# Polysketch attention with hash routing on one core: 16-bit routing one-hots, tails in two products, the first batch in groups of four tiles, three buffers for q's features

## The chip, the cores and the metric

The kernel runs on one core of a Trainium2 chip. A core has five engines that run side by side[...]: TensorE (PE in the profile, with its weight loads as a row of their own, PEld), VectorE (DVE), ScalarE (ACT), GpSimd (POOL) and SyncE (SP). SP only issues DMAs here; POOL issues the indirect ones. The metric is the device time of one execution in microseconds (us). The kernel before took 212.41 us, the median of three runs (211.67 to 212.51). The profile is of one more execution, whose time was 205.21 us and whose instructions span 203.5 us. All starts and durations below are from that execution.

## What is computed

```python
# q, k, v: (4 batches, 4 heads, 1088 tokens, 32), S1, S2: (8, 32)
def phi(x):                         # 64 features of a token
    a = einsum('rd,bhsd->bhsr', S1, x)
    b = einsum('rd,bhsd->bhsr', S2, x)
    return einsum('bhsi,bhsj->bhsij', a, b).reshape(..., 64)
q_p, k_p = phi(q), phi(k)
kv  = einsum('bhsf,bhsd->bhfd', k_p, v)
z   = sum(k_p, axis=2)
num = einsum('bhsf,bhfd->bhsd', q_p, kv)
den = einsum('bhsf,bhf->bhs', q_p, z)[..., None] + 1e-6
x   = (num / den).transpose(0, 2, 1, 3).reshape(4352, 128)

expert = token_ids * 2654435761 % 8           # one expert of 8 for a token
for e in range(8):
    mask = expert == e
    out[mask] = relu(x[mask] @ w1[e]) @ w2[e] # (128 -> 1024 -> 128)
```

The multiplier is 1 modulo 8, so a token's expert is its id's last three bits.

## The kernel before, in words

**Names.** P is 128. A batch has T = 8 main tiles of 128 tokens and a tail of SP = 64 tokens. The tails of the four batches lie together in one tile, two to each half of the partitions. Q = 4 tiles form a group; GQ = 2 groups are a batch. FB = 2: the 64 features of a head are handled as two blocks of 32 (D) for q. DA = 33 is a head's 32 values and a one, which makes the denominator come out beside the numerator. ST = 36 lists of 128 tokens each hold the routed tokens (18, HT, from the early part of the tokens and 18 from all), and C = 34 is how many tokens a partition holds in the routing.

**Stage 1, attention, about 0 to 71 us.** For each batch b the engines do this, with the code's helpers named:

- SP loads k, q and v (`load_main`), two batches deep, and the tails (`load_tail`, four DMAs for each of k, v and q). The loads for all batches are issued from one list at the top, in the order k0, q0, v0, k1, the tails of k and v, q1, the tail of q, v1, and so on. SP takes them in order[...].
- PE turns k by transposing it against an identity (`transposed`, L353), ACT copies the result out of PSUM; PE multiplies with S (`k_products`, L362), ACT copies again (`copied`, L379). DVE forms k's features by a broadcast product (`k_features`, L385).
- DVE turns q in 32 by 32 blocks (`q_blocks`, L440), PE multiplies with S (`q_products`, L362), ACT copies, DVE forms q's features and turns them (`q_features` L385 and `q_turned` L460). Features of q live in tiles `fT`, two buffers.
- PE sums features times values over the eight tiles and the tail (`kv_products`, L413). ACT copies the diagonal blocks of the result in 16 pieces of 32 by 66 into the block matrices `m` (`kv_diagonal`, L434), which have zeros elsewhere. In the last batch, kv is first copied to SBUF (`kv_both`), and the 16 pieces are shared: 8 on ACT, 8 on DVE.
- PE multiplies q's features with `m` (`x_products`, L469), eight times for each group, and the tail of a batch by eight products that contract over only 32 rows each (`x_tail_products`, L480). fp32 products run as two passes on PE, so the profile counts two matmuls for each. ACT copies to `xe` (L472, L483). DVE takes reciprocals of the denominators (L493, L494), and POOL, for one batch in the middle and part of the last DVE, multiplies (`x_main`, L499; `x_tail`, L513) and SP writes the rows to a DRAM scratch, `x_rows`.

The routing is woven in on DVE: `route_scan` and `route_counts` in the first batch, `route_ranks` and `route_slots` in batch 0's loop, then `route_rows(b)` (L314), a one-hot of 128 columns for half of the 34 tokens of a partition, once in each of batches 0 and 1, and `route_tiles` (L318 to L321) after the loop: a one-hot of 36 columns, scaled by the partition number and by the column number. PE contracts row and tile one-hots into the list of tokens (`route_list`, L327). `route_end` makes the row numbers `get` and `put` of it.

**Stage 2, the handover, about 55 to 74 us.** The first six gathers of rows from `x_rows` (`fetch(0)`, `fetch(1)`, L586) are issued by POOL. They need `get` and the rows of the first two batches and of the first half of batch 2. `bring(k)` transposes three gathered tiles on PE (L627).

**Stage 3, the experts, 71.8 to 196 us.** 16 groups of 288 tokens: PE does `layer1` (L690) and `layer2` (L697) of neighbouring groups in turn, ACT and DVE evict, POOL gathers and scatters. `bring(1)` comes after the fourth of the eight products of the first group, `bring(2)` in the second group.

**What sets the order.** There is no planner: everything runs under a manual schedule, so each engine runs its instructions in the order in which the program lists them. A helper that is called earlier moves all that it issues forward on each of its engines, past what the others have queued there. Buffers turn in pools (`bufs=`): a tile that takes a used buffer waits for that buffer's readers. `keep_busy` (L178) issues idle matmuls at the start, WARM = 7 of them ahead of the first transposes.

Of the kernel before, what the change touches and what calls it, by code (L numbers as in the profile page):

```python
# [30 lines left out]
def kernel(  # L31
# [38 lines left out]
    WARM = 7  # L70
# [6 lines left out]
    hots = tc.alloc_tile_pool(name="hots", bufs=1)  # L77
    ps = ctx.enter_context(tc.tile_pool(name="ps", bufs=4, space=bass.MemoryType.PSUM))
# [18 lines left out]
    def load_tail(src, name, eng):  # L97
        t = const.tile([P, H, TT, D], F32, name=name)
        for b in range(B):
            u = b % 2  # L100
            eng.dma_start(t[u * SP:(u + 1) * SP, :, b // 2], src[b, :, SM:, :].rearrange("h p d -> p h d"))
        return t
# [16 lines left out]
    def load_batch(b):  # L119
        k_t.append(load_main(k, b, "k"))  # L120
        q_t.append(load_main(q, b, "q"))
        v_t.append(load_main(v, b, "v"))
# [17 lines left out]
    q_tail = load_tail(q, "q_tail", nc.sync)  # L140
# [6 lines left out]
    warm = const.tile([P, 512], BF16)  # L147
# [5 lines left out]
    for t in range(Q):  # L153
# [7 lines left out]
                            fill=0.0, base=0, channel_multiplier=-1)  # L161
    keep = const.tile([P, E, C], F32)
# [9 lines left out]
    def keep_busy(n):  # L172

        if n == 0:
            return
        p = ps_o.tile([P, 512], F32, tag="o", name="idle")
        for _ in range(n):
            nc.tensor.matmul(p[:], warm[:, 0:P], warm[:], start=True, stop=True)  # L178
# [6 lines left out]
    xes = [const.tile([P, GQ * H * Q + H, DA], F32, name=f"xe{i}") for i in range(2)]  # L185
    for m in ms[0] + ms[1]:
        nc.vector.memset(m[:], 0.0)
# [62 lines left out]
    st = const.tile([P, 2, C], F32)  # L250
# [35 lines left out]
    def route_slots():  # L286
# [22 lines left out]
        nc.vector.tensor_copy(st[:], st_i[:])  # L309


    def route_rows(part):
        c = slice(part * C // 2, (part + 1) * C // 2)
        nc.vector.tensor_tensor(row1[:, c], iota[:].unsqueeze(1).to_broadcast([P, C // 2, P]),  # L314
                                st[:, 1, c].unsqueeze(2).to_broadcast([P, C // 2, P]), op=OP.is_equal)

    def route_tiles():
        nc.vector.tensor_tensor(in_tile[:], iota[:, 0:ST].unsqueeze(1).to_broadcast([P, C, ST]),  # L318
                                st[:, 0].unsqueeze(2).to_broadcast([P, C, ST]), op=OP.is_equal)
        nc.vector.tensor_scalar(tiles[:, :, 0], in_tile[:], p1[:], None, op0=OP.mult)  # L320
        nc.vector.tensor_tensor(tiles[:, :, 1], in_tile[:], iota[:, 0:C].unsqueeze(2).to_broadcast([P, C, ST]),  # L321
                                op=OP.mult)
# [51 lines left out]
    def copied(ab_ps, rows=P, n=T):  # L374

        ab = work.tile([P, T, H, 2, R], F32, tag="ab", name="ab", bufs=3)
        for g in range(0, n, Q):
            w = min(Q, n - g)
            nc.scalar.copy(ab[:rows, g:g + w].rearrange("p t h x r -> p t h (x r)"),  # L379
                           ab_ps[:rows, g // Q, :, 0:w].rearrange("p h t y -> p t h y"))  # L380
        return ab
# [6 lines left out]
    def k_features(ab, n, pool, tag):  # L388

        kp = pool.tile([P, n, H, R, R], F32, tag="kp" + tag, name="kp" + tag, bufs=1)  # L390
        for g in range(0, n, Q):
            features(kp[:, g:min(n, g + Q)].rearrange("p t h i j -> p (t h) i j"),
                     ab[:, g:min(n, g + Q)].rearrange("p t h x r -> p (t h) x r"))
        return kp

    def values(vsrc, n, pool, tag, copy=nc.gpsimd.tensor_copy):
# [3 lines left out]
        copy(va[:, :, :, 0:D], vsrc[:].rearrange("p h t d -> p t h d"))  # L400
        return va

    def kv_products(b, main, tail, midway=None):
        kv = ps_o.tile([P, H // 2, HA + 2 * DA], F32, tag="o", name="kv")
        u = b % 2
        steps = [(main, t, slice(0, P)) for t in range(T)] + [(tail, b // 2, slice(u * SP, (u + 1) * SP))]
        for n, ((kp, va), t, rows) in enumerate(steps):
            if midway and n == T // 2:
                midway()
# [8 lines left out]
        return kv  # L418

    def kv_diagonal(b, kv):  # L420

        m = ms[b % 2]
        kv = kv[:, :, 0:2 * DA]
        if b > EB:
# [3 lines left out]
            kv = both  # L428
        for f in range(FB):
            copy = nc.vector.tensor_copy if b > EB and f else nc.scalar.copy  # L430
            for h in range(2):
                src = kv[h * R * R + f * D:h * R * R + (f + 1) * D, :, h * DA:(h + 1) * DA]
                for t in range(Q):
                    copy(m[f][t * D:(t + 1) * D, h::2, t], src)  # L434
        return m
# [7 lines left out]
    def q_products(qT, n):  # L443

        ab_ps = bank([P, GQ, H, Q, 2 * R], "abq_ps")
        for g in range(0, n, Q):
            w = min(Q, n - g)
            for h in range(H):
                wide_products(ab_ps[:w * D, g // Q, h:min(h + 2, H)], qT[:, h, g:g + w].rearrange("p t s -> p (t s)"), s_k[:])
        return ab_ps  # L450

    def q_features(ab, g, r, pool, tag, bufs, eng=nc.vector):

        f = work.tile([P, Q, H, FB * D], F32, tag="f", name="f", bufs=1)
        features(f[r].rearrange("p q h (i j) -> p (q h) i j", i=R), ab[r, g * Q:(g + 1) * Q].rearrange("p q h x r -> p (q h) x r"), eng)
        return q_turned(f, r, pool, tag, bufs)

    def q_turned(f, r, pool, tag, bufs):
        fT = pool.tile([P, H * FB, P], F32, tag="fT" + tag, name="fT", bufs=bufs)
        nc.vector.transpose(fT[r].rearrange("p k (q s) -> p k q s", q=Q), f[r].rearrange("p q h (k d) -> p (h k) q d", d=D))  # L460
        return fT
# [12 lines left out]
    def x_tail_products(b, m):  # L474
        u, t = b % 2, b // 2
        rows, r = slice(u * SP, (u + 1) * SP), slice(t * D, (t + 1) * D)
        p = ps_x.tile([P, H, DA], F32, tag="x", name="x_ps")
        for h in range(H):
            for fb in range(FB):
# [495 lines left out]
```

## Time and profile before

| | busy us | share | what it is |
|---|---|---|---|
| PE | 191.6 | 94% | of it 160.7 in the experts' two lines, L690 and L697 |
| DVE | 114.0 | 56% | full from about 20 to 59 us |
| POOL | 92.3 | 45% | gathers, scatters, products of x |
| ACT | 69.6 | 34% | evictions from PSUM |
| DMA, SP's queue | | 38% | 20.98 MB |

A row of the page or of an answer gives the start and duration, the engine, the line, the operation, what it writes and reads, the shape, a count, and in brackets how long the engine had stood idle before it and what ended that. A row of the table of stretches gives for each engine its busy time within the stretch, with the number of instructions in brackets, in the order PE, PEld, DVE, ACT, POOL, and then the granted clock of TensorE, the mean busy share of the DMA engines and the GB/s moved. A busy share over the whole span mixes the attention, where several engines are full, with the experts, where PE alone is; the stretches tell them apart.

### The profile page before, as it was taken

To read this page: it belongs to the slowest core of one execution; us is meant where nothing else is said; L and a number is where in the kernel's file an instruction comes from. 1 tells how busy PE (TensorE), PEld (TensorE's weight loads), DVE (VectorE), ACT (ScalarE), POOL (GpSimd) and SP (SyncE) were. 2 spreads that over 40 slices of the span, in tenths; PEclk is the share of its full clock that TensorE was granted. 3 is DMA by queue.
4 is the path that set the end of the run, shared out by engine and by line. 5 is a ranking of instruction groups with operands and counts; after the bars stand their busy time and mean duration, and the time that the engine had idled before them with its cause. 6 is when DMAs were issued, how large, how long until landed. Compare 5 with 4: busy or idle time off the path is not lost. (4 is left out here: it accounts for less than half of the span.)

```text
span 203.5 us, 3365 instructions
## 1 busy us (share of the span) xinstructions
PE 191.6 (94%) x1126; PEld 159.8 (79%) x1126; DVE 114.0 (56%) x262; ACT 69.6 (34%) x210; POOL 92.3 (45%) x111
## 2 busy tenths in 40 slices
PE   7899969999988999999999999999999999999990
PEld 2699959899987887777777777777777777777980
DVE  7795999999999642223542443434434755423320
ACT  2362822842715432323322323313313223221330
POOL 6002201607305857317547277756677533114751
PEclk9999999999999999999999999999999999999997
DMA  5948999999911304203151423293223272210100
GB/s 127 294 87 224 333 360 338 342 371 343 343 58 50 102 27 147 51 13 92 52 103 42 103 65 93 64 119 72 69 77 90 51 103 53 51 49 21 43 30 21
DMA packets 39649, 25.82 MB, mean 127 GB/s; under 512 B 20698, under 2 KB 36827, under 8 KB 39632
## 3 DMA queue, kind: packets, MB, share of 16 engines
q1 hardware_dynamic: 37168, 20.98, 38.3%
q0 software_dynamic: 2304, 4.59, 8.1%
q8 instruction: 9, 0.15, 0.3%
q14 instruction: 8, 0.07, 0.1%
q10 hardware_dynamic: 160, 0.04, 0.1%
HBM read 17.47 MB, written 4.59 MB: 108 GB/s over the span
## 5 line engine op out<-in xcount | busy, mean ns | idle before, releaser
L690 PE MATMUL hp<-xT,w 128*128 128x288 f32 (+2 forms) x272 | 81.7, 393 | 0.0
L697 PE MATMUL op<-hT,w 128*128 128x288 f32 (+1 forms) x256 | 79.0, 399 | 0.0
L594 DVE TENSOR_SCALAR hT<-hp 128x288 f32<-128x288 f32 (+2 forms) x68 | 29.6, 439 | 64.7 <-PE hp L690 59.5
L690 PEld LDWEIGHTS hp<-xT,w 128*128 128x128 f32 x272 | 49.6, 190 | 12.8 <-issue 0.3
L700 POOL DMA_INDIRECT out_dram<-os,put x36 | 36.2, 1005 | 47.4 <-DVE os L752 28.0
L697 PEld LDWEIGHTS op<-hT,w 128*128 128x128 f32 x256 | 47.7, 190 | 12.5
L592 ACT ACTIVATE hT<-hp 128x288 f32<-128x288 f32 (+2 forms) x68 | 27.2, 401 | 67.3 <-PE hp L690 67.3
L586 POOL DMA_INDIRECT xg<-x_rows,get x36 | 38.1, 1058 | 21.2 <-DVE f L385 10.5
L499 POOL TENSOR_TENSOR xs<-xe,den 128x512 f32<-128x512 f32 x6 | 7.7, 1294 | 21.6 <-DVE den L494 12.1
L413 PE MATMUL kv<-va,kp 128*128 128x132 f32 x128 | 15.4, 277 | 0.5 <-DVE kp L385 0.5
L469 PE MATMUL x_ps<-m,fT 128*128 128x132 f32 x128 | 15.8, 280 | 0.0
L413 PEld LDWEIGHTS kv<-va,kp 128*128 128x128 f32 x128 | 14.8, 190 | 0.7 <-issue 0.7
L469 PEld LDWEIGHTS x_ps<-m,fT 128*128 128x128 f32 x128 | 14.8, 190 | 0.3
L731 ACT COPY half<-op 128x288 uint16<-128x288 uint16 (+1 forms) x26 | 9.1, 400 | 13.0 <-PE op L697 13.0
L434 ACT COPY m<-kv 32x66 f32<-32x66 f32 x48 | 9.9, 206 | 10.1 <-PE kv L413 9.5
L385 DVE TENSOR_TENSOR f<-ab 128x1024 f32<-128x1024 f32 (+1 forms) x9 | 11.6, 1290 | 0.5 <-ACT ab L379 0.3
L460 DVE STREAM_TRANSPOSE fT<-f 128x1024 f32<-128x1024 f32 (+1 forms) x9 | 11.2, 1244 | 0.7
L362 PE MATMUL abq_ps<-s_k,qT 128*128 128x128 f32 (+3 forms) x72 | 8.8, 275 | 1.2 <-DVE qT L440 1.2
L362 PEld LDWEIGHTS abq_ps<-s_k,qT 128*128 128x128 f32 (+1 forms) x72 | 8.3, 185 | 1.9 <-issue 1.4
L385 DVE TENSOR_TENSOR kp<-ab 128x1024 f32<-128x1024 f32 x8 | 9.3, 1195 | 0.0
L362 PE MATMUL ab_ps<-s_k,kT 128*128 128x128 f32 (+3 forms) x72 | 9.0, 276 | 0.0
L362 PEld LDWEIGHTS ab_ps<-s_k,kT 128*128 128x128 f32 (+1 forms) x72 | 8.5, 191 | 0.5
(144 smaller groups left out, 138.5 us busy)
## 6 DMA issues: line engine op xcount, KB each, us to landing
w<-in_moe_w_dram SPq DMA_DIRECT2D x16, 512.0 KB, 8.9
q<-in_q_dram SPq DMA_DIRECT2D x3, 512.0 KB, 7.3
k<-in_k_dram SPq DMA_DIRECT2D x3, 512.0 KB, 6.5
v<-in_v_dram SPq DMA_DIRECT2D x3, 512.0 KB, 5.7
x_rows<-xs SPq DMA_DIRECT2D x3, 512.0 KB, 6.6
xg<-x_rows,get POOLq DMA_INDIRECT x36, 2.7
out_dram<-os,put POOLq DMA_INDIRECT x36, 2.3
k<-in_k_dram SPq DMA_DIRECT2D x2, 256.0 KB, 3.4
```

Of the source, the lines that this page charges most:

```text
L362: nc.tensor.matmul(dst, stationary, s.rearrange("p t x r -> p t (x r)").unsqueeze(1).to_broadcast([s.shape[0], n, s.shape[1], 2 * R]), sta ...
L385: eng.tensor_tensor(dst, ab[:, :, 0].unsqueeze(3).to_broadcast(shape), ab[:, :, 1].unsqueeze(2).to_broadcast(shape), op=OP.mult)
L413: nc.tensor.matmul(kv[:].rearrange("p x y -> p (x y)")[:, pr * HA:(pr + 1) * HA], kp[rows, t, 2 * pr:2 * pr + 2].rearrange("p h i j -> p ( ...
L434: copy(m[f][t * D:(t + 1) * D, h::2, t], src)
L460: nc.vector.transpose(fT[r].rearrange("p k (q s) -> p k q s", q=Q), f[r].rearrange("p q h (k d) -> p (h k) q d", d=D))
L469: nc.tensor.matmul(p[:, h], fT[:, (h0 + h) * FB + fb], m[fb][:, h0 + h].rearrange("p t d -> p (t d)"), start=(fb == 0), stop=(fb == FB - 1 ...
L586: nc.gpsimd.indirect_dma_start(out=dst, out_offset=None, in_=x_dram[0:rows], in_offset=bass.IndirectOffsetOnAxis(ap=idx, axis=0), bounds_c ...
L592: nc.scalar.activation(dst, src, AF.Relu if relu else AF.Copy)
L594: return nc.vector.tensor_scalar(dst, src, 0.0, None, op0=OP.max).ins
L690: nc.tensor.matmul(hp[:, 0:hi - lo], w1[:, g % E, c * P:(c + 1) * P], x_columns(g * GN + lo, g * GN + hi), start=True, stop=True)
L697: nc.tensor.matmul(ops[g][:, 0:hi - lo], w2[:, g % E, c], hTs[g][:, c, lo:hi], start=(c == 0), stop=(c == FC - 1))
L700: st_ = nc.gpsimd.indirect_dma_start(out=out[:], out_offset=bass.IndirectOffsetOnAxis(ap=idx, axis=0), in_=src, in_offset=None, bounds_che ...
```

## The change

- **Routing.** The slot numbers `st` are written as bf16, each twice in a row. `route_rows` and the tile one-hot compare them, in pairs of two equal neighbours, with a bf16 `number` (`hot`). The product with the column number uses a bf16 `twice` in the same pairs. The product with the partition number moves from DVE to ACT (`route_tiles_p`). `route_tiles` moves from behind the loop into batch 0, after its `route_rows`.
- **Tails.** q's tail is laid out and turned so that two heads and both feature blocks fill the 128 partitions. Its features and their transpose have 512 elements to a partition where they had 1024 on half of the partitions. A batch's tail of x takes two products over 128 rows, with a block matrix of its own (`m_tail`, two ACT copies a batch), for eight over 32 rows.
- **First batch.** v is loaded ahead of q. k's products, their copies, the copy of v and k's features go by groups of four tiles. The products of kv are begun early, and go on between q's products, the counts and the k tail's products. The turns of batch 1's k move behind them. On DVE the turn of q0 stands between the two halves of k's features.
- **Buffers.** `fT` gets a pool of its own with three buffers.
- **Last batches.** The 16 pieces of the last diagonal are shared 6 on ACT, 5 on DVE, 5 on POOL. `fetch(0)` is issued after them, and not ahead of q's features and the diagonal.
- **Start.** Ten idle matmuls for seven, on a one-column tile that is read as 128 or 512 columns; the zero fills of `m` move from DVE to ACT.

```diff
-    WARM = 7
+    WARM = 10
+    feats = tc.alloc_tile_pool(name="feats", bufs=3)
...
     def load_batch(b):
         k_t.append(load_main(k, b, "k"))
+        if b == 0:
+            v_t.append(load_main(v, b, "v"))
         q_t.append(load_main(q, b, "q"))
-        v_t.append(load_main(v, b, "v"))
+        if b > 0:
+            v_t.append(load_main(v, b, "v"))
...
-    q_tail = load_tail(q, "q_tail", nc.sync)
+    q_tail = load_tail(q, "q_tail", nc.sync, 2)
...
-    st = const.tile([P, 2, C], F32)
+    st = const.tile([P, 2, C, 2], BF16)
...
+    def hot(dst, numbers, values):
+        _, n, w = dst.shape
+        nc.vector.tensor_tensor(dst.rearrange("p c (n x) -> p c n x", x=2),
+                                numbers.rearrange("p (n x) -> p n x", x=2).unsqueeze(1).to_broadcast([P, n, w // 2, 2]),
+                                values.unsqueeze(2).to_broadcast([P, n, w // 2, 2]), op=OP.is_equal)
...
-        nc.vector.tensor_tensor(row1[:, c], iota[:].unsqueeze(1).to_broadcast([P, C // 2, P]),
-                                st[:, 1, c].unsqueeze(2).to_broadcast([P, C // 2, P]), op=OP.is_equal)
+        hot(row1[:, c], number[:], st[:, 1, c])
...
+    def route_tiles_p():
+        nc.scalar.activation(tiles[:, :, 0], in_tile[:], AF.Copy, scale=p1[:])
...
     def kv_diagonal(b, kv):
+        copies = [nc.scalar.copy] * (2 * FB * Q)
         if b > EB:
             both = const.tile([P, H // 2, 2 * DA], F32, name="kv_both")
             nc.scalar.copy(both[:], kv)
             kv = both
+            copies = [nc.scalar.copy] * 6 + [nc.vector.tensor_copy] * 5 + [nc.gpsimd.tensor_copy] * 5
...
     def x_tail_products(b, m):
-        for h in range(H):
-            for fb in range(FB):
-                nc.tensor.matmul(p[rows, h], fT_tail[r, h * FB + fb, rows], m[fb][r, h, t],
-                                 start=(fb == 0), stop=(fb == FB - 1), skip_group_check=True,
-                                 tile_position=(r.start, rows.start))
+        for pr in range(H // 2):
+            nc.tensor.matmul(p[rows, 2 * pr:2 * pr + 2].rearrange("p h d -> p (h d)"), fT_tail[:, pr * TT + t, rows],
+                             m[:, pr].rearrange("p h d -> p (h d)"), start=True, stop=True, skip_group_check=True,
+                             tile_position=(0, rows.start))
...
         route_rows(b)
+        if b == 0:
+            route_tiles()
         kTs = [transposed(k_t[b + 2], g, Q) for g in range(0, T, Q)]
+        if b == 0:
+            route_tiles_p()
...
-    route_tiles()
...
     kv = kv_products(e, (kp, va), (kp_tail, va_tail))
+    fT = q_features(abq, 0)
+    last_m = kv_diagonal(e, kv)
     fetch(0)
-    fT = features_of(abq, 0)
-    last_m = kv_diagonal(e, kv)
     x_products(b, 1, fTs[1], m)
-    x_tail_products(b, m)
+    x_tail_products(b, m_tail)
+    m_tail = kv_tail(e, kv)
```

## Prediction

> **What bounds the kernel now.** All durations and starts are in us from the one profiled execution, whose span is 203.5. I read the table of busy time by stretch first, because the shares on the page average two different stages.
>
> ```profile
> core 0: us, PE busy (x) PEld busy (x) DVE busy (x) ACT busy (x) POOL busy (x), PEclk, DMA share, GB/s
> ...
> 20.00:28.00 8.00, 7.84 (x69) 7.51 (x67) 7.55 (x24) 5.56 (x23) 1.23 (x1) 1.00 1.06 336
> 28.00:34.00 6.00, 4.17 (x44) 4.15 (x45) 5.96 (x5) 1.59 (x4) 0.00 (x0) 1.00 1.10 353
> 34.00:41.00 7.00, 6.73 (x57) 6.34 (x56) 6.75 (x8) 4.53 (x20) 4.23 (x5) 1.00 1.12 339
> 41.00:50.00 9.00, 9.00 (x87) 8.71 (x86) 8.86 (x9) 2.92 (x8) 3.01 (x3) 1.00 1.10 359
> ...
> 60.00:100.00 40.00, 39.01 (x223) 32.11 (x222) 19.21 (x51) 13.75 (x40) 21.53 (x21) 1.00 0.24 68
> 100.00:150.00 50.00, 50.00 (x207) 39.00 (x206) 20.23 (x57) 14.88 (x40) 31.07 (x31) 1.00 0.39 81
> ```
>
> From 100 on PE never stops and DVE is 40% busy: the expert layers are PE's, and the change doesn't touch them. So what counts is when they start (71.79) and when their early inputs arrive. From 28 to 41 DVE has no gap while PE idles, so DVE leads there; from 41 to 60 both are full. The timeline then shows what DVE starts from and where it lets PE go.
>
> ```profile
> 19.77 1.25 DVE L440 STREAM_TRANSPOSE qT<-q 128x1024 f32<-128x1024 f32 x1 [2.27 <-DMA q<-in_q_dram]
> ...
> 27.21 1.21 DVE L385 TENSOR_TENSOR f<-ab 64x1024 f32<-64x1024 f32 x1
> 28.45 1.24 DVE L460 STREAM_TRANSPOSE fT<-f 64x1024 f32<-64x1024 f32 x1
> ...
> 31.86 2.41 DVE L314 TENSOR_TENSOR row<-iota,st 128x2176 bf16<-128x2176 f32 x1
> 34.19 0.18 DVE L493 TENSOR_SCALAR den<-xe 128x36 f32<-128x36 f32 x1
> ...
> 37.13 1.20 DVE L440 STREAM_TRANSPOSE qT<-q 128x1024 f32<-128x1024 f32 x1
> ...
> 38.39 2.00 PE L362 MATMUL abq_ps<-s_k,qT 128*128 128x128 f32 x16 [0.27 <-DVE qT L440]
> ```
>
> DVE waits 2.27 for batch 1's q and is then a closed chain to 38.3, where PE waits for it. That load is issued at 12.96, behind eight tail loads on SP's queue. The third view is the handover to the experts.
>
> ```profile
> 60.03 0.33 SPq L507 DMA_DIRECT2D x_rows<-xs  x1
> 62.38 0.27 ACT L427 COPY kv_both<-kv 128x132 f32<-128x132 f32 x1 [4.64 <-PE kv L413]
> 62.95 1.23 POOL L586 DMA_INDIRECT xg<-x_rows,get  x1 [10.50 <-DVE f L385]
> ...
> 65.79 1.82 POOL L586 DMA_INDIRECT xg<-x_rows,get  x1 [0.31 <-issue]
> ...
> 70.56 1.00 POOL L586 DMA_INDIRECT xg<-x_rows,get  x1 [0.30 <-issue]
> 71.79 2.21 PE L690 MATMUL hp<-xT,w 128*128 128x288 f32 x8
> ...
> 73.59 0.49 PEld L627 LDWEIGHTS xp<-ident,xg 128*128 128x128 f32 x3
> ```
>
> The write of x rows lands 2.0 after 60.03, and six gathers follow on POOL. The third lands 3.3 after 65.79 (69.1; PE uses it at 70.0), the sixth 2.7 after 70.56 (73.26; PE uses it at 73.59). So the gathers are only some 0.3 to 0.9 ahead of PE: a PE that comes earlier finds them late.
>
> [...] (2176 elements in 2.41, 1224 in 1.39 or 1.42 with one fp32 operand); it has no 16-bit pair. [...] the second line having 1.98 for work that takes 1.16 to 1.23 alone:
>
> ```profile
> 38.12 1.03 POOL L400 COPY va<-v 128x1024 f32<-128x1024 f32 x1
> 38.26 1.98 DVE L385 TENSOR_TENSOR f<-ab 128x1024 f32<-128x1024 f32 x1
> ```
>
> [...] sixteen 32-row tail loads take 1.00.
>
> **The change, part by part.**
>
> *First batch and warm-up.* Three more idle matmuls of 0.43 hold the first transposes from 4.63 to some 5.2[...]. v comes ahead of q, so q0 should land near 10.4 (v's second half did, 7.0 after 3.40) and not 8.5. From there PE has 1.25 of transpose and 8.7 of queued work, so batch 1's products start near 20.4, 1.1 later than 19.32. This costs nothing at the end: PE must wait for DVE anyway, at the tail features (before: 2.00) and at 38. Nor does it gain: DVE's chain starts from q1, whose place behind the eight tail loads is unchanged, so 19.77 stays. ACT's four zero fills (about 0.6 each, as a 128x512 copy) fit ahead of its first copy at 5.78.
>
> *Tails.* q's tail transpose has 512 elements for 256: +0.28. Features and turn have 512 for 1024: 0.65 twice (a 128x512 product takes 0.69) for the 2.41 between 27.21 and 29.62: -1.1. The key features start at 28.85. ACT pays two copies a batch of about 0.25 and five of 0.2 once. These end near 26.7 (kv 20.3, 3.5 of diagonal, 1.2 of other copies, 0.5, 1.05), before DVE wants them at 27.5. On PE sixteen passes (1.04) become four (0.25): -0.79 per batch.
>
> *One-hots.* [...] The tile one-hot and its product: 0.76 each for 1.39 and 1.42[...]. The scaled copy goes to ACT, 1.2 (va's 1024 took 1.05), where ACT is idle at 33. But both DVE operations move from 50.2 to before the denominators of batch 0: there DVE now pays 1.27 + 0.76 + 0.76 = 2.79 for 2.33. Its gain of 0.77 shrinks to 0.34: qT is done at 38.0 and PE goes on at 38.04 for 38.38. PE's whole gain before that is lost in the wait.
>
> *From 38.04.* PE has, in before's durations: q products 1.79, x 3.80, tail 0.25, transposes 0.83, kv 3.80 + 0.64, k 1.78, q 1.74, list 1.2, x 1.88, kv 3.80 + 0.64 = 22.15, ending at 60.2 for 62.26: -2.07. DVE follows, freed of 3.9 at 50 and 1.1 at 44; its key features are ready at 54.3 for PE's 56. ACT's diagonal ends before PE asks. The third buffer frees nothing I can see: before's buffers were already read when refilled.
>
> *Handover.* Five of the last diagonal's copies go to POOL, and the first fetch comes after them. They need kv_both, at 60.65. POOL shows no such copy; bounds are 0.15 (a 128x32 fill) and 0.395 (a 128x256 copy), and I take 0.23. So the gathers start at 60.65 + 5 x 0.23 + 0.31 = 62.1 for 62.95, though their rows have landed at 59.7 (the row product being 2.4 earlier). Behind them queue x of the last batch and all other gathers. The sixth lands 10.0 after the first (before 10.3; the 1.82 beside a DVE product moves to the first, whose 1.23 goes): 72.1, used at 72.25 for 73.59. PE's own path: two x pairs to 62.2; then the tail and the last batch's x wait for ACT's six diagonal copies (60.65 + 6 x 0.25 = 62.2) and two evictions of 0.38, so that x runs from 63.1 to 66.9 (3.8). There PE waits for the third gather, 6.1 after the first, 68.2. Its transposes (0.49) and ACT's eviction (0.49) let layer 1 start at 69.2; eight passes of 0.24 later, at 71.1, PE reaches the second three tiles and waits again, to 72.25.
>
> **Sum:** -1.3, the gathers deciding; span 202.2. The three timed runs (211.67 to 212.51) lie above the profiled run's 205.21; I carry the difference over unscaled: 212.41 - 1.3 = 211.1.
>
> **Rivals.**
> 1. *PE decides.* POOL's copies cost 0.1 each, gathers overlap better, or DVE releases PE earlier (q1 sooner). Then up to the 2.07 at kv, plus 0.8 of the last tail: -1.9 to -3, 209.4 to 210.5. For it: 0.8 to 1.6 of PE wait at the handover would vanish. Against it: kv_both itself lies ahead of the gathers.
> 2. *The gathers eat it all.* DVE's five copies (0.24 each) run in the same stretch; if they lock out POOL's five, these take 2.4 and the gathers start at 63.4. Or the first gather needs the 0.95 that it took after its rows landed. -0.5 to +0.5: 212.4. Against it: the second gather, beside such DVE copies, took 1.00 as always.
> 3. *Slower: no pair mode.* [...] qT is done at 40.4, kv at 62.6, the gathers start at 64.4 and end 0.9 to 1.3 later than now: 213.5. It decides from the point where these three take more than 4.1. [...]
> 4. *Slower: q1 lands later.* The same path, one for one, from 1.3 later on.
>
> **How the numbers follow.** Forecast case (-0.6 to -1.9, likeliest 211.1): 0.45. PE decides: 0.18. Eaten: 0.20. Slower by pair mode 0.08, by q1 or anything like it 0.09. Half a per cent, 1.06, is what a measurement of this kernel tells from no change. Faster by more: three quarters of the first and all of the second, 0.52. Within: the rest of the first and nearly all of the third, 0.30. Slower: 0.18. The range for 8 in 10 runs from the far end of PE deciding, 209.4, to a part of the slower cases, 213.4; the forecast case alone has 210.5 to 211.8.
>
> **What would show it.** Right: DVE's qT of batch 1 still starts near 19.8 after a wait for q; row one-hots near 1.3; PE waits for qT near 38 by over 1; kv_both near 60.4; five POOL copies ahead of a first gather near 62.1; PE idle before the first two transposes of gathered rows. Wrong: one-hots of 2.4, q1 landing far from 19.7, POOL copies over 0.4, or no PE wait at the handover.

## The result and the profile after

The first comparison gave 211.31 us (median of four runs) against 212.04 us for the kernel before, with a ratio of 0.9887 [0.9838, 0.9937]: faster, by about 1.1%. Two of the four runs (215.99 and 212.96) were disturbed, at lower granted clocks (0.968 and 0.985), and the ratio, which leaves such runs out, sets three runs (209.37 to 209.65, one of them beyond the four) against four of the kernel before (211.04 to 212.51). Two later comparisons of the same two kernels, with 22 runs of the changed kernel each, were made on another chip, as the 8 us less that the kernel before takes there suggest. They gave 203.51 against 204.01, ratio 0.9975 [0.9958, 0.9993], and 203.75 against 203.87, ratio 0.9984 [0.9965, 1.0002]. So the gain is 1.1% in the first comparison, from few runs, and about 0.2% on the second chip, at the edge of what the intervals can tell.

The forecast was 211.1, or -1.3 of 212.41. That the median came within 0.2 of it is luck: it is the middle between runs of 209.65 and 212.96. By the ratios the gain is 2.4 on the first chip, more than the forecast case allows (-0.6 to -1.9), and 0.3 to 0.5 on the second, less than it. The forecast lies between the two.

The first trace of the changed kernel is of the run of 215.99 (span 214.3), so the lines below are from its second trace, span 201.9 against 203.5 for the trace of before.

First the table of busy time by stretch, changed kernel (columns as in the prediction).

```profile
20.00:28.00 8.00, 7.94 (x69) 7.62 (x69) 7.46 (x24) 6.83 (x31) 1.04 (x1) 1.00 1.10 341
28.00:34.00 6.00, 6.00 (x54) 5.68 (x53) 5.93 (x9) 3.36 (x6) 0.15 (x1) 1.00 1.11 351
34.00:41.00 7.00, 6.15 (x53) 5.89 (x53) 6.86 (x6) 5.27 (x23) 4.08 (x5) 1.00 1.11 338
41.00:50.00 9.00, 9.00 (x78) 8.56 (x78) 8.83 (x10) 3.81 (x13) 5.03 (x5) 1.00 1.09 359
60.00:100.00 40.00, 37.85 (x186) 30.02 (x185) 18.17 (x43) 14.10 (x41) 24.22 (x28) 1.00 0.24 65
```

PE's idle time of 1.83 in 28 to 34 is gone, and 34 to 41 has it instead (0.85, before 0.27): PE comes to the q products earlier and waits there for DVE, as forecast. The last row holds the handover to the experts, and there PE idles 2.15 where it idled 0.99. The same can be read in the timeline, first up to that wait:

```profile
17.94 1.20 DVE L479 STREAM_TRANSPOSE qT<-q 128x1024 f32<-128x1024 f32 x1
20.05 0.71 DVE L503 STREAM_TRANSPOSE qT_tail<-q_tail 128x512 f32<-128x512 f32 x1 [0.91 <-DMA q_tail<-in_q_dram]
...
30.37 1.28 DVE L328 TENSOR_TENSOR row<-number,st 128x2176 bf16<-128x2176 bf16 x1
...
35.98 1.20 DVE L479 STREAM_TRANSPOSE qT<-q 128x1024 f32<-128x1024 f32 x1
37.24 2.00 PE L383 MATMUL abq_ps<-s_k,qT 128*128 128x128 f32 x16 [0.85 <-DVE qT L479]
```

The one-hot takes 1.28 for 2.41. Batch 1's q no longer makes DVE wait; the tail of q does. Then the handover, same trace:

```profile
57.65 0.69 DVE L573 TENSOR_TENSOR xs<-xe,den 128x512 f32<-128x512 f32 x1 [1.42 <-DMA x_rows<-xs]
59.52 0.27 ACT L457 COPY kv_both<-kv 128x132 f32<-128x132 f32 x1 [3.87 <-PE kv L442]
59.92 1.72 POOL L465 COPY m<-kv_both 32x66 f32<-32x66 f32 x5 [9.96 <-ACT kv_both L457]
61.93 1.23 POOL L668 DMA_INDIRECT xg<-x_rows,get  x1 [0.29 <-POOL m L465]
68.66 2.21 PE L775 MATMUL hp<-xT,w 128*128 128x288 f32 x8 [0.20 <-ACT xT L674]
71.70 0.33 PE L709 MATMUL xp<-ident,xg 128*128 128x128 f32 x1 [0.61 <-DMA xg<-x_rows,get]
```

kv_both is at 59.52 for 62.38, the first gather at 61.93 for 62.95, layer 1 at 68.66 for 71.79, and at 71.70 PE waits again for a gathered tile. Of 2.9 at kv_both and 3.1 at layer 1, 2.3 are left at the end of the first group (ACT's copy of it out of PSUM at 82.10 for 84.39) and 1.6 at the end of the span. At the copy of the last group it was still 2.45 (191.64 for 194.09); the last 0.8 is lost behind it. First the kernel before, then the changed one:

```profile
194.09 0.29 ACT L733 COPY late_cols<-op 128x160 f32<-128x160 f32 x1 [2.14 <-PE op L697]
198.61 0.98 POOL L700 DMA_INDIRECT out_dram<-os,put  x1 [0.70 <-ACT os L874]
```

```profile
191.64 0.29 ACT L818 COPY late_cols<-op 128x160 f32<-128x160 f32 x1 [2.14 <-PE op L782]
196.16 0.98 POOL L785 DMA_INDIRECT out_dram<-os,put  x1 [0.79 <-ACT os L959]
```

The last scatter starts 4.52 after that copy in both. From there the span runs on for 4.9 in the kernel before, in its second trace and in pairs_only below, and for 5.4 to 5.8 in all eleven traces of the changed kernel and its variants. So the changed kernel pays 0.5 to 0.9 at its very end; the traces don't show for what, and no run looked for it.

In the lines of the handover, the first has a wait that the forecast does not know: DVE stands 1.42 for the *store* of batch 1's rows, since the row buffer is single and must be read out before batch 2 writes into it.

### The profile page after: what moved, and what is told of

It is laid out like the page before. It is cut to its first block, busy times and chain, and to the rows that moved or that the text cites. A ratio compares the mean times of both kernels' runs of the same rounds, so it can differ in the third digit from the quotient of the medians.

```text
span 214.3 us, 3291 instructions
## 1 busy us (share of the span) xinstructions
PE 195.9 (91%) x1081; PEld 161.6 (75%) x1081; DVE 106.9 (50%) x256; ACT 74.4 (35%) x226; POOL 93.5 (44%) x118
## 5 line engine op out<-in xcount | busy, mean ns | idle before, releaser
L775 PE MATMUL hp<-xT,w 128*128 128x288 f32 (+2 forms) x272 | 82.9, 398 | 4.5 <-ACT hT L674 3.5
L782 PE MATMUL op<-hT,w 128*128 128x288 f32 (+1 forms) x256 | 80.4, 404 | 1.6 <-issue 1.0
L775 PEld LDWEIGHTS hp<-xT,w 128*128 128x128 f32 x272 | 50.0, 192 | 18.4 <-issue 2.7
L782 PEld LDWEIGHTS op<-hT,w 128*128 128x128 f32 x256 | 48.4, 192 | 14.9 <-issue 1.3
L668 POOL DMA_INDIRECT xg<-x_rows,get x36 | 37.1, 1031 | 11.4 <-issue 10.1
L544 PE MATMUL x_ps<-m,fT 128*128 128x132 f32 x128 | 19.1, 313 | 2.1 <-DVE fT L495 1.3
L544 PEld LDWEIGHTS x_ps<-m,fT 128*128 128x128 f32 x128 | 17.9, 222 | 2.7 <-ACT m_tail L473 1.5
L411 DVE TENSOR_TENSOR f<-ab 128x1024 f32<-128x1024 f32 x8 | 10.4, 1305 | 0.6 <-ACT ab L399 0.5
L495 DVE STREAM_TRANSPOSE fT<-f 128x1024 f32<-128x1024 f32 x8 | 10.0, 1245 | 0.5
L547 ACT COPY xe<-x_ps 128x264 f32<-128x264 f32 x16 | 6.0, 379 | 11.6 <-PE x_ps L544 9.1
L837 DVE COPY os<-turned 128x256 uint16<-128x256 uint16 (+1 forms) x26 | 7.7, 339 | 3.3 <-DMA turned<-half 3.3
```

Source lines behind the costliest of these rows:

```text
L411: eng.tensor_tensor(dst, ab[:, :, 0].unsqueeze(3).to_broadcast(shape), ab[:, :, 1].unsqueeze(2).to_broadcast(shape), op=OP.mult)
L495: nc.vector.transpose(fT[:].rearrange("p k (q s) -> p k q s", q=Q), f[:].rearrange("p q h (k d) -> p (h k) q d", d=D))
L544: nc.tensor.matmul(p[:, h], fT[:, (h0 + h) * FB + fb], m[fb][:, h0 + h].rearrange("p t d -> p (t d)"), start=(fb == 0), stop=(fb == FB - 1 ...
L668: nc.gpsimd.indirect_dma_start(out=dst, out_offset=None, in_=x_dram[0:rows], in_offset=bass.IndirectOffsetOnAxis(ap=idx, axis=0), bounds_c ...
L775: nc.tensor.matmul(hp[:, 0:hi - lo], w1[:, g % E, c * P:(c + 1) * P], x_columns(g * GN + lo, g * GN + hi), start=True, stop=True)
L782: nc.tensor.matmul(ops[g][:, 0:hi - lo], w2[:, g % E, c], hTs[g][:, c, lo:hi], start=(c == 0), stop=(c == FC - 1))
```

## The experiments

Ratios are to the kernel before on the same chip. Timed kernels of one group were compared there together.

**First group (chip with before at 204.01).** The changed kernel again, unedited:

> The changed kernel once more, for a profile to set beside the one at hand, in which TensorE's clock fell to 0.71 in the stretch 60 to 70 us and the expert layers stood still for some 5 us. Theory A (the handover decides): kv_both near 59.6 us, the row product of batch 2 held to near 59.5 us by the store of batch 1's rows, POOL's five copies 2.4 us, first gather near 63.1 us; layer 1 starts 0.5 to 1.5 us ahead of the 71.8 us of before, because the last x products now run at full clock. Rival B (the attention's saving arrives whole): layer 1 starts at 69.5 us or earlier. Time against before: A 0.988 to 0.996, B under 0.988.

Measured: 203.51, ratio 0.9975 [0.9958, 0.9993]; its lines are shown above. Neither case came as written: layer 1 came as early as in B (68.66), the first gather earlier than in A (61.93), and yet the time gained less than in either.

The pairs alone undone:

```diff
-    number = const.tile([P, P], BF16)
+    number = const.tile([P, P], F32)
-    twice = const.tile([P, C, 2], BF16)
+    twice = const.tile([P, C, 2], F32)
-    st = const.tile([P, 2, C, 2], BF16)
+    st = const.tile([P, 2, C, 2], F32)
```

> The changed kernel with the one-hots' numbers, slots and column numbers in fp32 (same pairs, same order)[...]. Row one-hot 2.4 us for 1.28, tile one-hot and column product 1.4 us each for 0.79. Batch 2's q products on PE start 2.3 to 2.5 us later (39.7 for 37.3 us). Theory A (the handover hangs on the store of batch 1's rows and on the gathers): PE's kv of the last batch ends up to 2.4 us later, and the gathers start with it, so the end moves by 0.5 to 2.4 us (ratio to the changed kernel 1.002 to 1.011). Rival C (DVE no longer matters after the move): no change within 0.3 us.

Measured: 208.41, ratio 1.0173 [1.0121, 1.0225]: 2.0% slower than the changed kernel, more than the 0.2 to 1.1% expected. From its timeline and its table by stretch:

```profile
29.62 2.42 DVE L328 TENSOR_TENSOR row<-number,st 128x2176 bf16<-128x2176 f32 x1
38.91 1.49 PE L383 MATMUL abq_ps<-s_k,qT 128*128 128x128 f32 x8 [2.94 <-DVE qT L479]
```

```profile
34.00:41.00 7.00, 4.06 (x29) 3.92 (x29) 6.83 (x8) 4.57 (x19) 4.23 (x5) 0.89 1.09 341
41.00:50.00 9.00, 9.00 (x73) 8.80 (x73) 8.75 (x9) 3.81 (x11) 2.23 (x2) 0.90 1.05 318
```

With fp32 operands the row one-hot is back at 2.42, and PE waits 2.94 for qT instead of 0.85. How much of it goes through is read best against the next kernel, no_pool_copies, in which q1 was there as early: qT of batch 3 comes 3.9 later (49.82 for 45.96), and three slower operations in batch 0 (2.4) and one in batch 1 (1.1) make up nearly all of it. kv_both is 4.1 later (62.82 for 58.74), layer 1 3.3 (72.49 for 69.22). So DVE leads this stretch and its operations count one for one. PE's granted clock also fell. It is 0.89 and 0.90 on the mean of the two stretches above, where the second trace of the changed kernel has 1.00, and the eight passes at 38.91 take 186 ns each where the sixteen at 37.24 there take 125. With DVE ahead as the limit, the slower PE cost little that this trace shows.

The last diagonal's copies off POOL:

```diff
-            copies = [nc.scalar.copy] * 6 + [nc.vector.tensor_copy] * 5 + [nc.gpsimd.tensor_copy] * 5
+            copies = [nc.scalar.copy] * 8 + [nc.vector.tensor_copy] * 8
```

> The changed kernel with the last diagonal's 16 pieces as before, 8 on ACT and 8 on DVE, none on POOL. Theory A: the gathers no longer wait for kv_both and POOL's 2.4 us; they start when the rows of batch 2 have landed, near 62.5 us (product near 59.5 us, store 2 us, start 1 us) for 63.1 us, so 0.6 us earlier; but DVE's eight copies and ACT's eight end later and x of the last batch with them. Net for layer 1: -0.6 to +0.6 us. Rival D (POOL's copies cost the end their whole 2.4 us): -1.5 us or more.

Measured: 202.86, ratio 0.9942 [0.9917, 0.9968], against 0.9975 for the unedited kernel; the intervals just overlap. The first gather starts at 61.28 for 61.93 though DVE's row product again waited (2.18, to 57.62). Layer 1 starts at 69.22, later than the 68.66 of the trace above, but PE then finds the second three tiles landed. By the medians POOL's five copies cost more than they relieve; the overlap leaves it open.

The weights of experts 4 to 7 behind the store of batch 1's rows, not ahead of it:

```diff
-        if b == 0:
+        if b == 1:
             load_experts(range(E // 2, E))
```

> The changed kernel with the loads of experts 4 to 7 listed in batch 1's turn of the loop, behind the store of batch 1's rows on SP's queue, and not in batch 0's. Theory A: the row product of batch 2 no longer waits 3.1 us on DVE for that store; it runs near 56.4 us for 59.5 us, the features behind it 3 us earlier, POOL's copies meet no long DVE product; first gather near 61.5 to 62.3 us for 63.1 us, layer 1 1 to 2 us earlier, time 0.5 to 1 per cent less than the changed kernel. Rival E (the store is not what holds the product): product still near 59.5 us, no change. The weights of experts 4 to 7 land later, but group 4 starts near 105 us.

Measured: 208.39, ratio 1.0203 [1.0155, 1.025]: 2.3% slower than the changed kernel, where 0.5 to 1% faster was expected. From the timeline (SPq is SP's queue of DMAs):

```profile
55.44 0.69 DVE L573 TENSOR_TENSOR xs<-xe,den 128x512 f32<-128x512 f32 x1
56.16 8.55 SPq L581 DMA_DIRECT2D x_rows<-xs  x2
65.38 1.23 POOL L668 DMA_INDIRECT xg<-x_rows,get  x1 [4.98 <-DVE xs_tail L587]
71.84 4.17 PE L775 MATMUL hp<-xT,w 128*128 128x288 f32 x8
```

The wait for batch 1's store is gone (55.44 with none), so the 4 MB ahead of that store made it; this half of the theory held. But now they stand ahead of batch 2's rows, issued at 56.16, and the first gather can't start before 65.38. POOL was free for five microseconds. The releaser that the line names, a DVE product of other rows, had ended 0.8 before (64.28 and 0.28 long); the store queued behind 4 MB is the likelier one, with the DMA engines full from 50 to 60 (a share of 1.09). The first transposes then wait 2.76, 1.02 and 0.79 for gathers, and layer 1's first eight passes take 4.17 for 2.21, the clock being 0.71 on the mean of 70 to 80.

**Second group (another chip, before at 209.87).** The kernel before once more, for a second trace, one run:

> The kernel before, unchanged, for a second trace of it. Both theories of q1 can be read here. If the landing of batch 1's q at 19.77 in the first trace was the order of the loads, DVE waits for it again until 19.5 to 20. If it was chance, DVE's transpose of it starts near 18 here too. Elsewhere the starts should repeat within 0.3: kv_both near 62.4, first gather near 62.95, layer 1 near 71.8.

Measured: 211.72. The first line below is from the first trace of the kernel before, the others from the second:

```profile
59.31 0.69 DVE L499 TENSOR_TENSOR xs<-xe,den 128x512 f32<-128x512 f32 x1
```

```profile
17.85 1.25 DVE L440 STREAM_TRANSPOSE qT<-q 128x1024 f32<-128x1024 f32 x1 [0.60 <-DMA q<-in_q_dram]
...
59.24 0.69 DVE L499 TENSOR_TENSOR xs<-xe,den 128x512 f32<-128x512 f32 x1 [1.73 <-DMA x_rows<-xs]
```

q1 landed 1.9 earlier than in the first trace of the same kernel, so 19.77 was one landing among several and not a property of the order of loads. DVE's chain was then early by as much, qT of batch 2 at 35.42 for 37.13, and it all ended in the same wait for batch 1's store: the row product at 59.24 for 59.31, the first gather at 62.89 for 62.95, layer 1 at 71.44 for 71.79. The wait on the store is older than the change; in the first trace it doesn't show, as DVE came late by itself.

The first batch as it was before, all else changed:

```diff
-    WARM = 10
+    WARM = 7
...
-        if b == 0:
-            v_t.append(load_main(v, b, "v"))
         q_t.append(load_main(q, b, "q"))
...
-    parts_ps = [k_products(kTs[g:g + 1], Q) for g in range(GQ)]
...
+    qT = q_blocks(q_t[0], T)
+    abk_ps = k_products(kTs, T)
+    abk = copied(abk_ps)
...
```

> The changed kernel with the first batch of the kernel before: loads in the order k, q, v, whole-batch products instead of groups of four, 7 idle matmuls, zero fills on VectorE; tails, one-hots, buffers and copies stay as changed. Theory (the prediction's step: the start costs and gains nothing): DVE's closed chain from q1 and q_tail decides, so if q1 lands at 18 as in the changed kernel's trace the time is the same within 0.3%, kv_both near 59.5. Rival (the start with v ahead of q is what made q1 land earlier, 17.9 for 19.77): DVE waits for q1 until 19.8 again, the tail features start 0.5 to 0.8 later, and the time is 0.2 to 0.5% longer.

Measured: 209.29, ratio 0.9986 [0.9941, 1.0031]. q1 landed at 18.19 and qT of batch 2 came at 35.14, so the new start neither made q1 early nor gained on this path. The interval is too wide to exclude a few tenths of a per cent.

Two buffers for q's features:

```diff
-        fT = feats.tile([P, H * FB, P], F32, tag="fT", name="fT", bufs=3)
+        fT = feats.tile([P, H * FB, P], F32, tag="fT", name="fT", bufs=2)
```

> The changed kernel with two buffers for the turned q features instead of three. Theory (the prediction's step: the third buffer frees nothing): same within 0.2%, no DVE wait for PE ahead of an fT in the trace. Rival (the third buffer lets DVE turn batch 2's second half before PE has read batch 1's): a DVE wait for PE's x products of 0.3 or more appears near 57, and kv_both or the x rows of batch 2 come later; 0.1 to 0.5% slower.

Measured: 209.72, ratio 0.9956 [0.9903, 1.0009]. No DVE instruction that writes an fT waits for PE in its trace; layer 1 starts at 67.88. The third buffer frees nothing that this run could tell.

No POOL copies, and the weights of experts 4 to 7 late:

```diff
-        if b == 0:
-            load_experts(range(E // 2, E))
...
     x_tail(e, nc.gpsimd)
+    load_experts(range(E // 2, E // 2 + 1))
...
+    for i, gc in enumerate(((1, 0), (2, 6), (3, 6))):
+        at(*gc, load_experts, range(E // 2 + 1 + i, E // 2 + 2 + i))
```

> The changed kernel with two edits: none of the last diagonal's copies on POOL (8 on ACT, 8 on DVE), and the weights of experts 4 to 7 loaded after the last x rows (expert 4) and beside groups 1 to 3 (the others) instead of at batch 0's rows. Theory (the store of batch 1's rows queues behind these 4 MB, and its landing is what holds DVE's row product of batch 2 at 57.6): that wait of 1.4 to 2.2 vanishes, the row product starts near 56, the first gather starts near 60 to 61, layer 1 near 68 or before, and the time is below that of the version without POOL copies alone (ratio to the kernel before 0.985 to 0.993). Rival (the wait is harmless, since kv_both and the copies come later anyway): no wait, but the first gather still starts near 61.3 and the ratio stays at 0.994. Third: late loads collide with gathers or with SP's transposes in the expert layers: slower than the version without POOL copies.

Measured: 209.81, ratio 0.9992 [0.9943, 1.0041]. The mechanism did what the theory says: the row product at 55.36 with no wait, the first gather at 60.21, layer 1 at 67.00, the earliest of its group. The time did not follow.

```profile
80.87 0.33 PE L707 MATMUL xp<-ident,xg 128*128 128x128 f32 x1 [1.23 <-DMA xg<-x_rows,get]
```

The loads fill the DMA engines to 0.90 of their time in 70 to 80, and just after it a gather makes PE wait 1.23, where the unedited kernel's second trace has no such wait. The first group's copy out of PSUM is at 82.21, no earlier than in that kernel (82.10, on the other chip). So the third expectation, collision, fits the trace; the version without POOL copies alone, against which it was to be slower, was not timed on this chip.

**Third group (the first group's chip, before at 203.87).** No POOL copies, as in no_pool_copies, and of the weights only those of experts 6 and 7 late:

```diff
-            load_experts(range(E // 2, E))
+            load_experts(range(E // 2, E - 2))
...
+    for e, gc in ((E - 2, (2, 6)), (E - 1, (3, 6))):
+        at(*gc, load_experts, (e,))
```

> The changed kernel with no copies of the last diagonal on POOL (8 on ACT, 8 on DVE) and with the weights of experts 6 and 7 alone taken out of the load at batch 0's rows and issued beside groups 2 and 3 instead; experts 4 and 5 stay. Theory (the store of batch 1's rows lands when the traffic queued ahead of it is done, and holds DVE's row product of batch 2): with 2 MB less ahead of it that wait, 1.4 to 2.2, vanishes; the row product starts near 55.4, the first gather near 60.2, layer 1 near 67, as with all four experts late, and without that version's 1.8 of waits for the second three tiles, since no weights run beside those gathers: first evictions of group 0 near 79.5 to 80, ratio to the kernel before 0.4 to 1.0% below that of the unedited changed kernel on the same chip. Rival (any earlier start is given back in the expert layers whatever the traffic): layer 1 near 67, but the ratio no better than the unedited one's within 0.2%.

Measured: 203.46, ratio 0.9976 [0.9957, 0.9996], against 0.9984 [0.9965, 1.0002] for the unedited kernel beside it: not told apart, as the rival had it. Nor is it better than no_pool_copies alone was in the first group (0.9942 [0.9917, 0.9968]), so moving the weights shows no gain in time. The row product is at 55.94 with no wait, layer 1 at 67.93 for 70.17 and the first group's copy at 81.22 for 82.77. But the first gather starts only at 61.56, 4.9 after the store of its rows was issued (4.0 in the next kernel); what held it isn't settled by the trace. By the trace 1.0 of the lead is left at the last group (191.35 for 192.32); the timed runs show 0.3.

The same, and one tile product moved:

```diff
     def route_tiles():
         hot(in_tile[:], number[:, 0:ST], st[:, 0])
+
+    def route_tiles_c():
         nc.vector.tensor_tensor(tiles[:, :, 1].rearrange("p c (n x) -> p c n x", x=2),
...
             fTs.append(q_features(abq, 1))
+    route_tiles_c()
```

> As split_weights, and the product of the tile one-hot with the column number (0.80 on DVE) moved from batch 0, ahead of the denominators, to after batch 1's q features, ahead of DVE's wait of 2.1 for ACT's copies. Theory: there it lies in that wait and is free; in batch 0 DVE's closed chain ends 0.8 earlier, qT of batch 2 with it, and PE goes on 0.8 earlier from 38; with the store out of the way 0.3 to 0.8 of it reaches layer 1; 0.1 to 0.4% faster than split_weights. Rival (what holds the handover is ACT's diagonal and the gathers, not PE's time from 38): same as split_weights within 0.15%.

Measured: 202.43, ratio 0.9930 [0.9905, 0.9955], the fastest of all: its interval lies below those of split_weights (by a hair) and of the unedited kernel. Compared over the two groups it is not told apart from no_pool_copies (0.9942 [0.9917, 0.9968]), which leaves store and product as they were. The product took 0.75 at 46.44 and DVE's wait for ACT's copies after it shrank from 2.1 to 0.77, so it cost nothing there. In batch 0 qT came at 34.48, ahead of PE, which did not wait at all in 34 to 41. Row product, kv_both and gathers moved with it. The unedited kernel's trace is set against it here, first the unedited one:

```profile
58.31 0.69 DVE L573 TENSOR_TENSOR xs<-xe,den 128x512 f32<-128x512 f32 x1 [2.65 <-DMA x_rows<-xs]
59.37 2.42 POOL L465 COPY m<-kv_both 32x66 f32<-32x66 f32 x5 [9.96 <-ACT kv_both L457]
62.55 0.46 PE L544 MATMUL x_ps<-m,fT 128*128 128x132 f32 x2 [0.85 <-DVE fT L495]
63.83 5.43 PE L544 MATMUL x_ps<-m,fT 128*128 128x132 f32 x30 [0.81 <-DVE m L465]
```

And split_tiles:

```profile
55.11 0.69 DVE L575 TENSOR_TENSOR xs<-xe,den 128x512 f32<-128x512 f32 x1
59.83 1.23 POOL L671 DMA_INDIRECT xg<-x_rows,get  x1 [11.74 <-DVE fT L497]
61.51 2.07 PE L546 MATMUL x_ps<-m,fT 128*128 128x132 f32 x16
63.79 2.04 PE L546 MATMUL x_ps<-m,fT 128*128 128x132 f32 x16 [0.22 <-DVE den L569]
```

In the unedited kernel the store held DVE for 2.65; DVE's products then fell beside POOL's copies, which took 2.42; PE waited 0.85 and 0.81 for DVE; and its thirty passes took 181 ns each for 129, with the clock at 0.83 on the mean of 60 to 70 (1.00 in split_tiles). In split_tiles, with neither the store's wait nor POOL's copies, the same work runs through; these lines don't part the two. By the last group 0.5 is left in the traces (191.79 for 192.32), because split_tiles met a stop of 1.9 in the sixth group, where DVE waited 2.67 for a DMA transpose of results. The traced run is the slowest of its seven (203.47, the others 201.71 to 203.30), so that stop need not come in every run.

One part of the change alone, in the kernel before:

```diff
-        nc.vector.tensor_tensor(row1[:, c], iota[:].unsqueeze(1).to_broadcast([P, C // 2, P]),
-                                st[:, 1, c].unsqueeze(2).to_broadcast([P, C // 2, P]), op=OP.is_equal)
+        hot(row1[:, c], number[:], st[:, 1, c])
```

(and likewise for the two tile operations; the scaled one stays on DVE)

> The kernel before with one part of the change alone: the one-hots in 16-bit pairs, each where it was, the scaled one on DVE as before. Theory: DVE saves 1.13 in batch 0 and 1.13 in batch 1, so PE goes on 1.1 earlier at 38; the tile one-hots save 1.25 more near 50; but the store of batch 1's rows still holds the row product of batch 2 to 57.5 or later, so that first gather and layer 1 come only 0.3 to 1.2 earlier: ratio 0.993 to 0.999. Rival (the 2% lost when the pairs alone were undone is what the pairs are worth anywhere): ratio 0.980 to 0.986.

Measured: 203.52, ratio 0.9972 [0.9954, 0.9989]: as expected, and not told apart from what the whole change gave beside it. So on this chip the time shows nothing of the change beyond its pairs. kv_both is at 60.34 (60.67 in the second trace of before), the row product waits 1.41 for batch 1's store, to 58.45, the first gather is at 62.09, layer 1 at 70.92. The pairs are worth 0.3% alone and 2% when they are taken out of the changed kernel. The traces say the same ahead of the expert layers: at the first group's copy 0.5 to 0.9 (83.53 for 84.04 and 84.39) and 3.6 (82.10 for 85.73). The changed kernel has three such operations, not one, ahead of qT of batch 2, and in the kernel before a part of the gain runs into the store. The rival, one price anywhere, is refuted.

The unedited kernel beside them:

> The changed kernel unedited, for the comparison on this chip: 0.2 to 1.2% faster than the kernel before, as on the two chips before; row product of batch 2 at 57.5 to 59.5 after a wait for the store of batch 1's rows, first gather 62 to 63, layer 1 68.5 to 72.

Measured: 203.75, ratio 0.9984 [0.9965, 1.0002]; its lines are shown above.

## Why the prediction was right, and where not

The time was right by the luck told of above. Of the mechanism, the size of the one-hots, PE's wait for qT (0.85, forecast over 1) and the gathers as the last limit (in one of two traces) came as forecast; two steps of the path to them failed. Two of the signs named for being wrong came as well: q1 landed far from 19.7, and POOL's copies took over 0.4 each on the mean in three traces.

**The one-hots** were sized rightly: 1.28, 0.79 and 0.80 for the forecast 1.27, 0.76 and 0.76, and 1.32 on ACT for 1.2. That 16-bit pairs would halve the time was the author's estimate, which no line of the trace of before showed; the runs nearly show it for these shapes (1.28 for 2.42 in no_pairs, 0.79 and 0.80 for 1.43). So the third rival, the three operations at 2.41 + 1.39 + 1.42 = 5.2 as before and not at 2.79, did not occur, and no_pairs shows what it would have cost. The forecast put it 0.9 to 1.3 above the kernel before. At the end of the first group that is what the traces show (85.73 for 84.39, +1.3). The timed loss is 1.7%, some 3.5: the trace of no_pairs has a stop of 1.4 more in the sixth group, and 0.8 more between ACT's last copy and the end, as the changed kernel itself has. So the rival's path was sized rightly, and its time was not.

**PE from 38.04, 22.15 of work.** Measured from 37.24 to 59.42, 22.2. This part of the sum held to 0.1; only its start was 0.8 earlier.

**"19.77 stays" failed.** In the second trace of before and in all eleven of the changed kernel and its variants DVE has q1 by 18.4 (in pairs_only by 19.22, after a wait that the trace puts down to PE). Reading one landing time off one trace and treating it as fixed was the error; before_again showed the scatter, 1.9, in the unchanged kernel.

**"Rows landed at 59.7, the row product being 2.4 earlier" failed.** DVE was ready for that product at 56.2 but had to wait for the store of batch 1's rows, to 57.65, 58.31 and 59.46 in the three traces. The forecast listed what every moved step issues but did not ask what traffic stands ahead of a store that frees a buffer. The sum was there to be made: q, k and v are 6.7 MB, the weights 8.4, the rows of two batches 1.1, together 16.2 MB (from the shapes), and the table shows the DMA engines full from 20 to 50 at 338 to 359 GB/s. At 340 that is 48 us of transfer, most of it ahead of this store. That the place in the queue counts is shown by store_first: there the store moved ahead of the 4 MB ended DVE's wait (55.44 with none), and with the next one behind them the first gather came at 65.38.

**POOL's copies: 0.23 each was right, their sum was not.** A copy by itself takes 0.23 to 0.24, but five take 1.36 with the gaps between them (no_pairs, store_first; 1.35 in feats2) for the forecast 1.15, and 1.72 to 2.42 in four other traces. There one copy of the five is long. In the first trace of the changed kernel it is the last, 1.22 from 61.17, and DVE's product of q's features runs from 61.08 to 62.29: the copy ends 0.1 after it. In after_third, where the five take 2.42, the third starts at 59.93 and takes 1.30 (2.42 less four of 0.23 and their gaps), and such a product runs from 59.92 to 61.13. In the second trace of the changed kernel and old_start too the long copy ends 0.1 after such a product. DVE's own copies show no such thing: in no_pairs and store_first they run beside POOL's five, which take 1.36. So the second rival's figure of 2.4 came, but not from the five DVE copies that it named. In the traces with the longest store waits (3.13, 2.65, 2.58) DVE's product met the copies as it had been made late by the store.

**The handover.** First gather forecast 62.1, measured 61.93 and 62.08; layer 1 forecast 69.2, measured 68.66 and 70.17; PE waits before the sixth tile in one trace, as forecast, and not in the other, where PE itself was late. Errors of opposite sign met: kv_both was 0.9 earlier than thought (done at 59.79 for 60.65), and the five copies took 0.6 longer (1.72 for 1.15). So the sum of -1.3, against -1.6 and -1.2 in the spans, is right in size partly by chance.

**Tails, start and third buffer.** PE's tail products take 0.45 for 1.11 (forecast -0.79, measured -0.66). On ACT the tail copies ended later than DVE wanted them: DVE waited 0.58 to 1.45 for them in nine of eleven traces, where the forecast had 0.8 to spare: an earlier q1 brings DVE there earlier, but not ACT. So in these traces DVE's chain starts from ACT's tail copies, near 26, and not from q1. Start and third buffer were put at nothing; old_start and feats2 show no effect their intervals could tell. No run took the tails out alone.

**The size in time.** The first trace of before (205.21) was set against timed runs at 212.41, and the difference carried over. It fits the chip of the first group better, where it would lie 1.2 above the median; the record doesn't name its chip. A gain read against that trace then looks larger than the 0.3 to 0.5 timed there. Why the first comparison shows 1.1% is not settled. Its runs of before lie 8 above the other chip's, and the first trace of the changed kernel has stops in the expert layers that the second has not (PE waits 2.12 at 134.95 for ACT); no experiment was made on them.

## What to carry to other kernels

When a change speeds up what leads a stage, look for the buffer whose reuse waits on a *store*, and add up the bytes queued ahead of that store. Taking the wait away is not yet a gain: 2 MB of weights moved away ended it and showed nothing in time. With 0.8 of DVE work put into an existing wait as well, and POOL's copies given back, the kernel reached 0.7% instead of 0.2%; POOL's copies given back alone reached 0.6% in another comparison, so what each part adds is open.

An operation is worth what stands behind it: the same pairs gave 0.3% in one schedule and 2% in another. Don't take a landing time from one trace as a constant.

## What was not expected of the hardware

- The granted TensorE clock fell, down to half, after short waits of PE. In the first trace of the changed kernel it was 0.58 from 64 to 65, 0.50 from 65 to 70, 0.51 from 70 to 71 and 1.00 after that, behind waits of 0.34, 1.35 and 0.71 within some 3.3 us; the thirty passes there took 6.59 for 3.87 (at 129 ns each). After waits of 0.34, 0.85 and 0.81 in after_third they took 5.43, at a mean of 0.83 from 60 to 70. After one wait of 2.94 in no_pairs the means were 0.89 and 0.90 from 34 to 41 and 41 to 50. After one of 2.12, at 134.95 in the first trace of the changed kernel, it was 0.50 from 136 to 139, with 0.92 and 0.88 in the microseconds beside them.
- A small copy on POOL (32 by 66, fp32) took 0.23, also beside copies and transposes on DVE, and up to 1.30 in the four traces in which it began beside a DVE product of two inputs.
- All traces have the same period of 7.76 for a group in the expert layers; they differ by single stops, groups that take longer. The largest are 1.9 in the sixth group and 3.4 in the seventh; the seventh stops only on the second group's chip and in the first trace of the changed kernel, in the kernel before as well. What makes them stays open.
